# Attention, a Sinkhorn mixture of experts and a top-1 mixture: half blocks in two passes in the second mixture's expert layers, with wider weight splits and moved transposes

## Chip, cores and metric

One core of one Trainium2 chip. The metric is the device time in microseconds of one execution, as the median of several runs. The profile is of one execution, whose own time is given beside its span.

## What is computed

The reference, cut to what matters here: a windowed attention gives `x` (1536 tokens of 512), a first mixture of 8 experts with Sinkhorn weights gives a new `x`, and the second mixture sends each token to one expert:

```python
# attention: B, H, S, D = 2, 8, 768, 64, window 128 with 4 sinks
x = moe_sinkhorn(x)                     # N, D, E, F = 1536, 512, 8, 1024
logits = x @ w_gate
expert_idx = np.argmax(logits, axis=1)
gate_w = softmax(logits)[np.arange(N), expert_idx]
for e in range(E):
    mask = expert_idx == e
    h = np.maximum(x[mask] @ w1[e], 0.0)          # 512 -> 1024
    out[mask] = gate_w[mask, None] * (h @ w2[e])  # 1024 -> 512
```

## The kernel before, in words

The precision of a float32 product is reached with fp32r matmuls: each operand is split into a high part (a rounded copy) and a low part (the rest). `mm3` (line 65) computes a product in three passes, low x high, high x low and high x high, all added up in one PSUM bank.

Attention runs to about 200 us of the span and the first mixture to about 1230 us. In the last part of the first mixture, jobs that run beside its matmuls (`start`, `tick`) route the tokens of the second one: `route_tile` and `route_chunk` find the expert of each token, `pick` takes the fullest expert of the first third of the tokens, `first_tables` fills its two blocks of 128 tokens, and `route_dynamic` (line 569) lays out everything else on VectorE, when all tokens are routed.

The second mixture works on blocks of 128 gathered tokens, called items. Items 0 and 1 belong to the fullest expert. After them come 5 pairs of items (`NPAIR`), each pair with one expert's weights, and 6 single items (`NONE`), each with weights of its own, in the order single, pair, single, pair, and so on: items 2, 5, 8, 11, 14 and 17 are singles, 3 and 4 a pair. These 18 items (`NSURE`) always run; those whose place no tokens need still cost the same. One more single stands behind `tc.If(more == 1)` at the end (line 1448) and runs only when the tokens need it. Which expert an item has is known only at run time: the load's address is read from `ex_i` by SP.

For each item, `gather` (line 695) fetches rows of `x2d` by an indirect DMA from GpSimd, `xs_trans` (703) transposes them on TensorE, ScalarE writes the high part and VectorE the low one. `m2_l1` (714) computes one half (512 columns) of the first layer, and its result is evicted with the ReLU by ScalarE (half 0) or VectorE (half 1). `h_trans` (730) transposes the result in 2 x 4 pieces, again with a high part by ScalarE (L740) and a low part by VectorE (L741). `m2_l2` (744) computes the second layer in 8 steps of three matmuls; ScalarE scales by the gate weight (L757) and an indirect DMA scatters the rows into `out` (L758).

An expert's weights are 4 tiles of 1 MB. SP loads them into 4 raw buffers (`item_load`, line 796). `item_split` and `w_split` (155) split a tile in four pieces of 512 columns, a ScalarE copy (L166) and a VectorE subtraction (L168) each, into one of 7 slots (`SLOTS`, line 128). When a tile is split, the load of the tile four places later starts. `spend(n)` (line 766) issues n pieces, and stops early where the next tile's slot still has matmuls to come; `ensure` issues what a matmul cannot do without. The order is written out by hand, on each engine as the program says (`manual_schedule`):

```python
for i in range(2, NSURE):           # line 1426; shortened
    drain(m2_l1(i + 1, 0)); h_trans(i); gather(i + 3); spend(3)
    drain(m2_l1(i + 1, 1)); spend(3)
    xs_trans(i + 2); spend(3)
    drain(m2_l2(i)); spend(3)
```

Ahead of this loop, items 0 to 2 run with `tick()` between their steps; a job `early(16)` issues split pieces from there, and `spend(8)` stands just before the loop.

Of the kernel before, what the change touches and what calls it, by code (L numbers as in the profile page):

```python
# [23 lines left out]
def kernel(  # L24
# [30 lines left out]
    NITEM = NSURE + 1  # L55
    LAST = 2 * NPAIR + NONE
    ND = 2 * (LAST // 2 + 1)

# [47 lines left out]
    FIRST = {0: 0, 1: 0, NSURE: NSURE}  # L106
    COL = {NSURE: LAST}
    for u in range(NONE):
        FIRST[2 + 3 * u] = 2 + 3 * u
        COL[2 + 3 * u] = 2 * NPAIR + u  # L110
    for t in range(NPAIR):
        for j in range(2):
            FIRST[3 + 3 * t + j] = 3 + 3 * t
            COL[3 + 3 * t + j] = 2 * t + j

# [8 lines left out]
    SEQ += [(NSURE, r) for r in range(4)]  # L124
# [30 lines left out]
    def w_split(p, pool_lo=0):  # L155
        sl, r = w_slot(p)
        th, tl = (f"xh{r}", f"xl{r}") if sl == "x" else (f"wh{sl}{r}", f"wl{sl}{r}")
        h = pools[sl].tile([128, FB, 512], F32R, name=th)
        l = pools[sl].tile([128, FB, 512], F32R, name=tl)
        w_t[p] = h, l  # L160
        raw = raw_t.pop(p)
        for j in range(FB):
            if j == FB - 1 and pool_lo:
                nc.vector.tensor_copy(h[:, j, :], raw[:, j, :])
# [3 lines left out]
            eng.tensor_tensor(l[:, j, :], raw[:, j, :], h[:, j, :].bitcast(F32), op=ALU.subtract)  # L168
            yield
# [392 lines left out]
    def dyn_consts():  # L562
        sk = pools["s"]
        dynj["thr"] = sk.tile([128, NT], F32, name="thr")
        iota(dynj["thr"], [[128, NT]], 0, 0)
        dynj["j"] = sk.tile([128, ND + 1], F32, name="jio")
        iota(dynj["j"], [[128, ND + 1]], 0, 0)

    def route_dynamic():
        sk, psb = pools["s"], pools["ps"]  # L570
        thr, jio = dynj["thr"], dynj["j"]
        re = sk.tile([128, E], F32, name="re")
        nc.vector.tensor_tensor(re, counts, s8, op=ALU.subtract)
        shb = [128, E, NT]
        gt = sk.tile(shb, F32, name="gt")
        nc.vector.tensor_tensor(
            gt, re.unsqueeze(2).to_broadcast(shb), thr.unsqueeze(1).to_broadcast(shb), op=ALU.is_gt
        )
        ds = sk.tile([128, 2, E], F32, name="ds")
        nb = sk.tile([128, E], F32, name="nb")  # L580
        nc.vector.tensor_reduce(ds[:, 0, :], gt[:, :, 1::2], axis=AX.X, op=ALU.add)
        nc.vector.tensor_reduce(nb, gt, axis=AX.X, op=ALU.add)
        nc.vector.scalar_tensor_tensor(ds[:, 1, :], ds[:, 0, :], -2.0, nb, op0=ALU.mult, op1=ALU.add)
        see = [128, 2, E, E]
        tn = sk.tile(see, F32, name="x2h")
        nc.vector.tensor_tensor(
            tn, t8.unsqueeze(1).to_broadcast(see), ds.unsqueeze(2).to_broadcast(see), op=ALU.mult
        )
        ci = sk.tile([128, 2, E], F32, name="ci")
        nc.vector.tensor_reduce(ci, tn, axis=AX.X, op=ALU.add)  # L590
        yield
        d, s1, di = ds[:, 0, :], ds[:, 1, :], ci[:, 0, :]
        dt = sk.tile([128, 4], F32, name="dt")
        nc.vector.tensor_reduce(dt[:, 0:1], di, axis=AX.X, op=ALU.max)
        nc.vector.tensor_scalar(dt[:, 1:2], dt[:, 0:1], 2.0, float(2 * NPAIR), op0=ALU.mult, op1=ALU.max)
        nc.vector.tensor_scalar(dt[:, 2:3], dt[:, 0:1], 2.0, -2.0 * LAST, op0=ALU.mult, op1=ALU.add)
        pv_, al, hi = (sk.tile([128, E], F32, name=nm) for nm in ("sp", "sal", "shi"))
        nc.vector.scalar_tensor_tensor(pv_, ci[:, 1, :], dt[:, 1:2], s1, op0=ALU.add, op1=ALU.subtract)
        nc.vector.tensor_scalar(al, pv_, 2.0, dt[:, 2:3], op0=ALU.mult, op1=ALU.add)
        nc.vector.tensor_scalar(hi, al, float(2 * NPAIR), float(LAST), op0=ALU.is_ge, op1=ALU.mult)  # L600
        nc.vector.tensor_tensor(al, al, hi, op=ALU.max)
        nc.vector.tensor_tensor(al, al, pv_, op=ALU.subtract)
        nc.vector.scalar_tensor_tensor(hi, pv_, float(LAST), al, op0=ALU.is_ge, op1=ALU.mult)
        nc.vector.tensor_tensor(pv_, pv_, hi, op=ALU.add)

        b0, b1, b2 = (sk.tile([128, E], F32, name=nm) for nm in ("b0", "b1", "b2"))
        nc.vector.tensor_scalar(b1, di, 256.0, None, op0=ALU.mult)
        nc.vector.scalar_tensor_tensor(b0, d, -256.0, b1, op0=ALU.mult, op1=ALU.add)
        nc.vector.tensor_scalar(pv_, pv_, 128.0, 65536.0, op0=ALU.mult, op1=ALU.add)
        nc.vector.tensor_tensor(b2, pv_, s1, op=ALU.mult)  # L610
        nc.vector.tensor_scalar(b2, b2, -65536.0, None, op0=ALU.add)
        se = [128, ND, E]
        jb = jio[:, 0:ND].unsqueeze(2).to_broadcast(se)
        g0 = sk.tile(se, F32, name="g0")
        g1 = sk.tile(se, F32, name="g1")
# [8 lines left out]
        nc.vector.tensor_scalar(mo_i, ex[:, LAST:LAST + 1], 0.5, None, op0=ALU.is_gt)  # L624
        nc.vector.tensor_scalar(ex, ex, -1.0, float(E), op0=ALU.mult, op1=ALU.add)
        nc.vector.tensor_scalar(ex_i, ex, float(E - 1), None, op0=ALU.min)
        for n in range(4, 8):
            item_load(n)
        start(early(16), 10)
# [21 lines left out]
        sg = [128, NT, ND + 1]  # L651
        G = sk.tile(sg, F32, name="G")
        nc.vector.tensor_tensor(
            G, sd.unsqueeze(2).to_broadcast(sg), jio.unsqueeze(1).to_broadcast(sg), op=ALU.is_ge
        )
        jn = sk.tile([128, NT], F32, name="jn")
        nc.vector.tensor_reduce(jn, G[:, :, 1:ND + 1], axis=AX.X, op=ALU.add)
        nc.vector.scalar_tensor_tensor(sd, jn, -128.0, sd, op0=ALU.mult, op1=ALU.add)
        yield
        J = G[:, :, 0:ND]  # L660
        nc.vector.tensor_tensor(J, J, G[:, :, 1:ND + 1], op=ALU.subtract)
        nh = NT // 2
        sj = [128, nh, ND]
        As = [sk.tile([128, nh, 3, ND], F32R, name=nm) for nm in ("x2h", "x2l")]
        for u, A in enumerate(As):
            us = slice(u * nh, (u + 1) * nh)
            for j, g in enumerate((idp1[:, us], ghl[:, us, 0].bitcast(F32), ghl[:, us, 1].bitcast(F32))):
                eng = nc.gpsimd if u == 1 and j > 0 else nc.vector
                eng.tensor_tensor(A[:, :, j, :], J[:, us], g.unsqueeze(2).to_broadcast(sj), op=ALU.mult)
        tp = psb.tile([128, 3 * ND], F32, name="tabd", tag="m1")  # L670
        Rs = [onehots(sd[:, c * TPC:(c + 1) * TPC]) for c in range(2)]
        yield 2
        for c in range(NC):
            cols = [As[b // nh][:, b % nh].rearrange("p j e -> p (j e)") for b in range(c * TPC, (c + 1) * TPC)]
            place(tp, Rs[c], cols, c == 0, c == NC - 1)
            if c + 2 < NC:
                Rs.append(onehots(sd[:, (c + 2) * TPC:(c + 3) * TPC]))
            if c == 1:
                yield 1
        finish(tp, ND, ig_d, is_d, g_d)  # L680
        for i in range(2, 5):
            gather(i)

# [3 lines left out]

    def index(st, dy, i):
        return st[:, i:i + 1] if i < 2 else dy[:, COL[i]:COL[i] + 1]

# [4 lines left out]
    def gather(i):  # L695
# [3 lines left out]
            out=x, out_offset=None, in_=src, in_offset=bass.IndirectOffsetOnAxis(ap=index(ig_s, ig_d, i), axis=0)  # L699
# [3 lines left out]
    def xs_trans(i):  # L703
        x = xs_t.pop(i)
        tp = pools["ps"].tile([128, KD, 128], F32, name="xst", tag="m0")
        for kk in range(KD):
            nc.tensor.transpose(tp[:, kk, :], x[:, kk * 128:(kk + 1) * 128], ident)
# [4 lines left out]
        xst[i] = th, tl  # L712

    def m2_l1(i, hf):
# [5 lines left out]
        for kk in range(KD):  # L720
            mm3(ps, th[:, kk, :], tl[:, kk, :], wh[:, kk, :], wl[:, kk, :], kk == 0, kk == KD - 1)
# [22 lines left out]
    def m2_l2(i):  # L744
        pool, tag = ((ps_m, "y0"), (pools["ps"], "m2"))[i % 2]
        ps = pool.tile([128, DM], F32, name="y", tag=tag)
        for f in range(2 * FB):
# [4 lines left out]
            mm3(ps, th[:, f % FB, :], tl[:, f % FB, :], wh[:, f % FB, :], wl[:, f % FB, :], f == 0, f == 2 * FB - 1)  # L752
# [738 lines left out]
```

## Time and profile before

| what | value |
|---|---|
| median of 3 runs | 1462.15 us (1461.98 to 1463.06) |
| the profiled execution | 1461.6 us |
| its span, first to last instruction | 1459.8 us |
| TensorE busy, share of the span | 98% |
| VectorE, ScalarE, GpSimd busy | 47%, 31%, 9% |
| mean granted TensorE clock | 0.995 of full speed |

The span is what the profiler saw of the program; the time is longer by the start and the end of the execution. Matmuls are pipelined, so that the duration of one (some 390 ns) is longer than the step from one to the next. PE is TensorE, PEld its weight loads, DVE VectorE, ACT ScalarE, POOL GpSimd, SP the engine that issues the loads; a "q" behind the name is the engine's queue.

### The profile page before, as it was taken

To read this page: it belongs to the slowest core of one execution; us is meant where nothing else is said; L and a number is where in the kernel's file an instruction comes from. 1 tells how busy PE (TensorE), PEld (TensorE's weight loads), DVE (VectorE), ACT (ScalarE), POOL (GpSimd) and SP (SyncE) were. 2 spreads that over 40 slices of the span, in tenths; PEclk is the share of its full clock that TensorE was granted. 3 is DMA by queue.
4 is the path that set the end of the run, shared out by engine and by line. 5 is a ranking of instruction groups with operands and counts; after the bars stand their busy time and mean duration, and the time that the engine had idled before them with its cause. 6 is when DMAs were issued, how large, how long until landed. Compare 5 with 4: busy or idle time off the path is not lost. (4 is left out here: it accounts for less than half of the span.)

```text
span 1459.8 us, 18270 instructions
## 1 busy us (share of the span) xinstructions
PE 1426.6 (98%) x7181; PEld 1169.4 (80%) x7181; DVE 687.8 (47%) x1445; ACT 457.9 (31%) x974; POOL 125.5 (9%) x164
## 2 busy tenths in 40 slices
PE   7799999999999999999999999999999998999998
PEld 5587887888888888888888888888888876788886
DVE  7677644543333323233333323243333367877774
ACT  5766522021121212022111202112111132766664
POOL 3644400000000000000000000000000000111111
PEclk9999999999999999999999999999999999999999
DMA  6322112010101001010100001010100041977771
GB/s 131 76 59 53 37 58 87 0 58 1 58 8 51 29 29 58 1 58 0 58 30 29 29 30 58 0 58 1 58 1 0 30 144 44 352 278 266 267 256 52
DMA packets 86026, 105.64 MB, mean 72 GB/s; under 512 B 41519, under 2 KB 41519, under 8 KB 85937
## 3 DMA queue, kind: packets, MB, share of 16 engines
q1 hardware_dynamic: 83056, 96.58, 20.3%
q0 software_dynamic: 2880, 7.87, 1.6%
q8 instruction: 57, 0.93, 0.3%
q14 instruction: 33, 0.26, 0.1%
HBM read 101.29 MB, written 7.86 MB: 75 GB/s over the span
## 5 line engine op out<-in xcount | busy, mean ns | idle before, releaser
L201 ACT ACTIVATE hh<-L 128x512 fp32r<-128x512 f32 x192 | 114.7, 597 | 794.9 <-PE L L68 794.8
L202 DVE SCALAR_TENSOR_TENSOR hl<-L,hh 128x512 fp32r<-128x512 f32 x192 | 132.7, 691 | 345.6 <-ACT hh L201 344.9
L226 DVE SCALAR_TENSOR_TENSOR acc<-y,Pm,acc 128x512 f32<-128x512 f32 x168 | 126.1, 751 | 252.3 <-PE y L68 251.9
L66 PE MATMUL y<-whb,hl 128*128 128x512 f32 x432 | 170.7, 395 | 0.0
L68 PE MATMUL y<-whb,hh 128*128 128x512 f32 x432 | 168.5, 390 | 0.0
L67 PE MATMUL y<-wlb,hh 128*128 128x512 f32 x432 | 168.1, 389 | 0.0
L66 PE MATMUL y<-wha,hl 128*128 128x512 f32 x412 | 162.9, 395 | 0.0
L68 PE MATMUL y<-wha,hh 128*128 128x512 f32 x412 | 160.5, 390 | 0.0
L67 PE MATMUL y<-wla,hh 128*128 128x512 f32 x412 | 160.4, 389 | 0.0
L66 PE MATMUL L<-xh,wla 128*128 128x512 f32 x384 | 152.3, 397 | 0.0
L66 PE MATMUL L<-xh,wlb 128*128 128x512 f32 x384 | 151.0, 393 | 0.0
L68 PE MATMUL L<-xh,wha 128*128 128x512 f32 x384 | 149.6, 390 | 0.0
L68 PE MATMUL L<-xh,whb 128*128 128x512 f32 x384 | 149.6, 389 | 0.0
L67 PE MATMUL L<-xl,wha 128*128 128x512 f32 x384 | 149.6, 389 | 0.0
L67 PE MATMUL L<-xl,whb 128*128 128x512 f32 x384 | 149.5, 389 | 0.0
L68 PEld LDWEIGHTS y<-whb,hh 128*128 128x128 f32 x432 | 81.1, 188 | 17.3
L67 PEld LDWEIGHTS y<-wlb,hh 128*128 128x128 f32 x432 | 81.2, 188 | 16.0
L66 PEld LDWEIGHTS y<-whb,hl 128*128 128x128 f32 x432 | 81.1, 188 | 16.0
L698 POOL DMA_INDIRECT acc<-x2d,ig_s x2 | 2.1, 1052 | 1044.7 <-DVE tmp_d L449 1019.6
L68 PEld LDWEIGHTS y<-wha,hh 128*128 128x128 f32 x412 | 77.3, 188 | 16.3
L66 PEld LDWEIGHTS y<-wha,hl 128*128 128x128 f32 x412 | 77.3, 188 | 16.3 <-issue 0.3
L67 PEld LDWEIGHTS y<-wla,hh 128*128 128x128 f32 x412 | 77.4, 188 | 15.0
(311 smaller groups left out, 2328.6 us busy)
## 6 DMA issues: line engine op xcount, KB each, us to landing
raw<-in_moe_w SPq DMA_DIRECT2D x80, 1024.0 KB
raw<-in_v SPq DMA_DIRECT2D x12, 256.0 KB
raw<-vfb SPq DMA_DIRECT2D x12, 256.0 KB
x2d<-acc SPq DMA_DIRECT2D x12, 256.0 KB
raw<-in_k SPq DMA_DIRECT2D x11, 256.0 KB
raw<-in_q SPq DMA_DIRECT2D x11, 256.0 KB
raw<-in_k SPq DMA_DIRECT2D x2, 128.0 KB
raw<-in_q SPq DMA_DIRECT2D x2, 128.0 KB
```

What stands on the lines that cost most here:

```text
L66: nc.tensor.matmul(out_ap, al, bh, start=start, stop=False)
L67: nc.tensor.matmul(out_ap, ah, bl, start=False, stop=False)
L68: nc.tensor.matmul(out_ap, ah, bh, start=False, stop=stop)
L201: nc.scalar.activation(hh, ps, AF.Relu)
L202: nc.vector.scalar_tensor_tensor(hl, ps, 0.0, hh.bitcast(F32), op0=ALU.max, op1=ALU.subtract)
L226: nc.vector.scalar_tensor_tensor(a, ps, Pm[:, blk, e:e + 1], a, op0=ALU.mult, op1=ALU.add)
L698: nc.gpsimd.indirect_dma_start(out=x, out_offset=None, in_=src, in_offset=bass.IndirectOffsetOnAxis(ap=index(ig_s, ig_d, i), axis=0))
```

## The change

Of the 6 single items the last five (5, 8, 11, 14, 17) become half items of 64 rows. A half item's high and low parts lie side by side in one tile, 64 columns each, so that one matmul gives high rows in partitions 0 to 63 and low rows in 64 to 127; two passes, with the low and the high part of the weights, take the place of three, and `both` adds the two halves of the bank. The ReLU of a half item moves behind the transposes. The gather, the transposes and the scatter of a half item have 64 rows.

Routing counts remainders over 128 (a pair), over 64 (a full single) and up to 64 (a half). What does not fit goes to up to five pairs in nested branches at the end, in place of the one single; for this the tables are made by functions that can run again (`table_experts`, `tables`; their operations are those of before, with 16 columns instead of 18).

Weight tiles from the fifth on are split in two pieces of 1024 columns. The transposes of item i + 1 are issued inside the second layer of item i, after 5 of its 8 steps. The diff, cut to its core:

```diff
+    NHALF = NONE - 1
+    NOVER = 5
+    NITEM = NSURE + 2 * NOVER
+    ND = 2 * NPAIR + NONE
+    HALF = {2 + 3 * u for u in range(1, NONE)}
...
-    def w_split(p, pool_lo=0):
+    def w_split(p, pool_lo=0, n=1):
...
-        for j in range(FB):
+        for j in range(0, FB, n):
+            js = slice(j, j + n)
...
-                nc.scalar.activation(h[:, j, :], raw[:, j, :], AF.Copy)
+                nc.scalar.activation(h[:, js, :], raw[:, js, :], AF.Copy)
...
     def xs_trans(i):
...
+        n = rows(i)
+        tp = pools["ps"].tile([128, KD, 128], F32, name="xst", tag="m0")[:, :, 0:n]
         for kk in range(KD):
+            nc.tensor.transpose(tp[:, kk, :], x[0:n, kk * 128:(kk + 1) * 128], ident[0:n, 0:n])
+        if i in HALF:
+            st = stile("xsh", i, [128, KD, 128], F32R)
+            nc.scalar.activation(st[:, :, 0:n], tp, AF.Copy)
+            nc.vector.tensor_tensor(st[:, :, n:128], tp, st[:, :, 0:n].bitcast(F32), op=ALU.subtract)
+            xst[i] = st, None
+            return
...
+    def mm(out_ap, ah, al, bh, bl, start, stop):
+        if al is not None:
+            mm3(out_ap, ah, al, bh, bl, start, stop)
+        else:
+            nc.tensor.matmul(out_ap, ah, bl, start=start, stop=False)
+            nc.tensor.matmul(out_ap, ah, bh, start=False, stop=stop)
+
+    def both(dst, ps):
+        nc.scalar.activation(dst, ps[64:128, :], AF.Copy)
+        nc.vector.tensor_tensor(dst, ps[0:64, :], dst, op=ALU.add)
...
     def m2_l1(i, hf):
...
-        if hf == 0 or i < 2 or i == NSURE - 1:
+        if i in HALF:
+            both(h[0:64, :], ps)
+        elif hf == 0 or i < 2 or i == NSURE - 1:
...
     def h_trans(i, hfs=(0, 1)):
...
+            if i in HALF:
+                hi = th[:, :, 0:n]
+                nc.scalar.activation(hi, tp, AF.Relu)
+                nc.vector.scalar_tensor_tensor(
+                    th[:, :, n:128], tp, 0.0, hi.bitcast(F32), op0=ALU.max, op1=ALU.subtract
+                )
...
     def m2_l2(i):
...
+        if i in HALF:
+            both(y, ps)
+            ps = y
         nc.scalar.activation(y, ps, AF.Copy, scale=index(g_s, g_d, i))
...
-        start(early(16), 10)
+        start(early(8), 10)
...
     def early(n):
         for _ in range(n):
             spend(1)
-            yield 1
+            yield 2
...
-        yield from w_split(P1 + n)
+        yield from w_split(P1 + n, n=1 if n < 4 else 2)
...
         while jobs:
             tick()
-        spend(8)
+        h_trans(2)
+        spend(4)
         for i in range(2, NSURE):
             if i + 1 < NSURE:
                 drain(m2_l1(i + 1, 0))
-                h_trans(i)
             if i + 3 < NSURE:
                 gather(i + 3)
-            if not tail:
-                spend(3)
+            spend(2 if i % 3 == 0 else 1)
             if i + 1 < NSURE:
                 drain(m2_l1(i + 1, 1))
-            spend(3)
+            spend(2)
             if i + 2 < NSURE:
                 xs_trans(i + 2)
-            if not tail:
-                spend(3)
+            spend(1)
             for n, _ in enumerate(m2_l2(i)):
-                if tail and n == 4:
+                if n == 4 and i + 1 < NSURE:
                     h_trans(i + 1)
-                    spend(16)
-            spend(3)
+            spend(1 if i < NSURE - 2 else 8)
-        more = nc.values_load(mo_i[0:1, 0:1], min_val=0, max_val=1)
-        with tc.If(more == 1):
+        more = nc.values_load(mo_i[0:1, 0:1], min_val=0, max_val=NOVER)
+        def over(t):
+            if t == NOVER:
+                return
+            with tc.If(more > t):
...
+                over(t + 1)
```

In `route_dynamic`, the arithmetic from the counts to `ex_i` goes from 32 VectorE operations to 29; after the gathers of items 2 to 4, five more compute the number of overflow pairs.

## Rows read from the trace of the kernel before

**Rows 1.** The page, busy tenths of 40 slices of the span:

```profile
PE   7799999999999999999999999999999998999998
GB/s 131 76 59 53 37 58 87 0 58 1 58 8 51 29 29 58 1 58 0 58 30 29 29 30 58 0 58 1 58 1 0 30 144 44 352 278 266 267 256 52
```

**Rows 2.** Busy time by stretch: stretch, us, engines, PEclk, DMA share, GB/s

```profile
1240.00:1260.00 20.00, 18.95 (x85) 14.85 (x86) 16.86 (x43) 10.80 (x20) 5.89 (x8) 0.91 0.94 335
1260.00:1280.00 20.00, 20.00 (x102) 16.77 (x101) 18.57 (x31) 17.11 (x34) 2.77 (x3) 1.00 0.98 346
...
1360.00:1380.00 20.00, 20.00 (x100) 16.67 (x99) 12.59 (x21) 12.38 (x24) 4.22 (x4) 1.00 0.75 260
```

**Rows 3.** Waits of PE, 1215 to 1460: us, times, longest; first and last of six

```profile
PE L L66 <- DVE acc L711: 2.0, 1, 2.0
...
PE rkp L409 <- DVE oh_all L402: 0.2, 1, 0.2
```

**Rows 4.** Timeline of PE: start us, us, engine, line, operation, out<-in, count

```profile
1437.97 0.60 PE L737 MATMUL h2p<-ident,hh 128*128 128x128 f32 x4
...
1438.77 0.47 PE L66 MATMUL L<-xh,acc 128*128 128x512 f32 x1
...
1450.66 0.39 PE L66 MATMUL y<-whb,hl 128*128 128x512 f32 x1
...
1453.16 0.39 PE L68 MATMUL y<-whb,hh 128*128 128x512 f32 x1
```

**Rows 5.** Timeline of POOL, two scatters of neighbouring items

```profile
1350.41 1.01 POOL L758 DMA_INDIRECT out<-acc,is_d  x1 [9.88 <-ACT acc L757]
...
1362.71 1.01 POOL L758 DMA_INDIRECT out<-acc,is_d  x1 [9.88 <-ACT acc L757]
```

**Rows 6.** Timeline of PE, matmuls with 54 moving columns

```profile
1247.55 0.74 PE L533 MATMUL tabd<-x2h,acc 128*128 128x54 f32 x6
1248.13 0.38 PE L533 MATMUL tabd<-x2l,acc 128*128 128x54 f32 x2
```

**Rows 7.** Timeline of DVE, first operation of the layout and the eviction behind it

```profile
1232.51 0.15 DVE L573 TENSOR_TENSOR re<-counts,s 128x8 f32<-128x8 f32 x1
...
1239.62 0.68 DVE L711 TENSOR_TENSOR acc<-xst,acc 128x512 fp32r<-128x512 f32 x1
```

**Rows 8.** Groups by line and shape, whole span: busy us, mean ns, idle before

```profile
L1019 DVE TENSOR_TENSOR xl<-pv,xh 64x256 fp32r<-64x256 f32 x48 | 20.0, 416 | 14.9 <-ACT xh L1206 13.7 <-PE tr L1158 0.6 <-PE L L1028 0.2
L1089 DVE TENSOR_TENSOR vsk<-acc,vsk 64x512 fp32r<-64x512 f32 x2 | 1.4, 686 | 0.4 <-ACT vsk L1088 0.4
L1088 ACT ACTIVATE vsk<-acc 64x512 fp32r<-64x512 f32 x2 | 1.2, 616 | 0.0
```

**Rows 9.** Timeline of all engines, end of item 2's first layer

```profile
1262.94 0.39 PE L68 MATMUL L<-whb,acc 128*128 128x512 f32 x1
...
1263.37 0.69 DVE L728 TENSOR_SCALAR hl<-L 128x512 f32<-128x512 f32 x1
```

**Rows 10.** Groups by line and shape, 1240 to 1460

```profile
L168 DVE TENSOR_TENSOR xl<-raw,xh 128x512 fp32r<-128x512 f32 x76 | 48.3, 683 | 16.1 <-ACT xh L166 16.1
L166 ACT ACTIVATE xh<-raw 128x512 fp32r<-128x512 f32 x76 | 42.2, 631 | 0.7 <-DMA raw<-in_moe_w 0.7
...
L741 DVE TENSOR_TENSOR hl<-h2p,hh 128x512 fp32r<-128x512 f32 x34 | 22.0, 686 | 13.7 <-ACT hh L740 13.7
```

**Rows 11.** Timeline of all engines, the end of the span

```profile
1453.63 0.69 ACT L757 ACTIVATE acc<-y,g_d 128x512 f32<-128x512 f32 x1 [4.80 <-PEq L1448]
1454.59 0.98 POOL L758 DMA_INDIRECT out<-acc,is_d  x1 [4.50 <-ACTq L1448]
```

**Rows 12.** Busy time by stretch, the landing of the last scatter

```profile
1455.00:1459.00 4.00, 0.00 (x0) 0.00 (x0) 0.00 (x0) 0.00 (x0) 0.57 (x1) 0.62 0.06 20
```

**Rows 13.** Instructions of the early branch, line 923, on DVE's queue

```profile
L923 DVEq COMPARE_BRANCH  x1: 67/67/67, 7.7 to 7.7; - x1
L923 DVEq EVENT_SEMAPHORE  x1: 21/21/21, 8.3 to 8.3; - x1
```

More of the change, by code (lines that the diff above doesn't have):

```diff
@@ L113 @@
             FIRST[3 + 3 * t + j] = 3 + 3 * t
-            COL[3 + 3 * t + j] = 2 * t + j
+            COL[3 + 3 * t + j] = NONE + 2 * t + j
+    for t in range(NOVER):
+        for j in range(2):
+            FIRST[NSURE + 2 * t + j] = NSURE + 2 * t
+            COL[NSURE + 2 * t + j] = 2 * t + j
+    HALF = {2 + 3 * u for u in range(1, NONE)}
     def whose(i, rs):
@@ L123 @@
     NHEAD = len(SEQ)
-    SEQ += [(NSURE, r) for r in range(4)]
+    SEQ += [(NSURE + 2 * t, r) for t in range(NOVER) for r in range(4)]
     place_of = {ir: n for n, ir in enumerate(SEQ)}
@@ new lines, in dtile @@
+        def dtile(shape, nm):
+            dynj[nm] = pools["s"].tile(shape, F32, name=nm)
+            return dynj[nm]
+        thr = dtile([128, 3, NT // 2], "thr")
+        for j, a in enumerate((128, 64, 0)):
+            iota(thr[:, j, :], [[256, NT // 2]], a, 0)
+        iota(dtile([128, ND + 1], "jio"), [[128, ND + 1]], 0, 0)
+        for j, (n, a, b) in enumerate(((1, 511, 514 + NONE - 6), (NHALF, 512, 506 + NONE - 6))):
+            for nm, x in (("lim", n), ("pb", 128 * a), ("cv", 128 * b)):
+                t = dtile([128, 2, E], nm) if j == 0 else dynj[nm]
+                nc.gpsimd.memset(t[:, j, :], float(x))
@@ L616, in route_dynamic, with table_experts @@
+    def table_experts(b0, b1, b2, off):
+        sk = pools["s"]
+        se = [128, ND, E]
+        jb = dynj["jio"][:, 0:ND].unsqueeze(2).to_broadcast(se)
+        g0 = sk.tile(se, F32, name="lgs0")
+        g1 = sk.tile(se, F32, name="lgs1")
+        if off:
+            for b in (b0, b1, b2):
+                nc.vector.tensor_scalar(b, b, -off, None, op0=ALU.add)
         nc.vector.tensor_tensor(g0, jb, b0.unsqueeze(1).to_broadcast(se), op=ALU.is_ge)
@@ L623, in route_dynamic, with tables @@
         nc.vector.tensor_reduce(ex, g0, axis=AX.X, op=ALU.add)
-        nc.vector.tensor_scalar(mo_i, ex[:, LAST:LAST + 1], 0.5, None, op0=ALU.is_gt)
         nc.vector.tensor_scalar(ex, ex, -1.0, float(E), op0=ALU.mult, op1=ALU.add)
         nc.vector.tensor_scalar(ex_i, ex, float(E - 1), None, op0=ALU.min)
+    def tables(sd):
+        sk, psb = pools["s"], pools["ps"]
+        jio = dynj["jio"]
+        sg = [128, NT, ND + 1]
+        G = sk.tile(sg, F32, name="G")
+        nc.vector.tensor_tensor(
+            G, sd.unsqueeze(2).to_broadcast(sg), jio.unsqueeze(1).to_broadcast(sg), op=ALU.is_ge
+        )
+        jn = sk.tile([128, NT], F32, name="jn")
+        nc.vector.tensor_reduce(jn, G[:, :, 1:ND + 1], axis=AX.X, op=ALU.add)
+        sr = sk.tile([128, NT], F32, name="sr")
+        nc.vector.scalar_tensor_tensor(sr, jn, -128.0, sd, op0=ALU.mult, op1=ALU.add)
+        yield
+        J = G[:, :, 0:ND]
+        nc.vector.tensor_tensor(J, J, G[:, :, 1:ND + 1], op=ALU.subtract)
+        nh = NT // 2
+        sj = [128, nh, ND]
+        As = [sk.tile([128, nh, 3, ND], F32R, name=nm) for nm in ("x2h", "x2l")]
+        for u, A in enumerate(As):
+            us = slice(u * nh, (u + 1) * nh)
+            for j, g in enumerate((idp1[:, us], ghl[:, us, 0].bitcast(F32), ghl[:, us, 1].bitcast(F32))):
+                eng = nc.gpsimd if u == 1 and j > 0 else nc.vector
+                eng.tensor_tensor(A[:, :, j, :], J[:, us], g.unsqueeze(2).to_broadcast(sj), op=ALU.mult)
+        tp = psb.tile([128, 3 * ND], F32, name="tabd", tag="m1")
+        Rs = [onehots(sr[:, c * TPC:(c + 1) * TPC]) for c in range(2)]
+        yield 2
+        for c in range(NC):
+            cols = [As[b // nh][:, b % nh].rearrange("p j e -> p (j e)") for b in range(c * TPC, (c + 1) * TPC)]
+            place(tp, Rs[c], cols, c == 0, c == NC - 1)
+            if c + 2 < NC:
+                Rs.append(onehots(sr[:, (c + 2) * TPC:(c + 3) * TPC]))
+            if c == 1:
+                yield 1
+        finish(tp, ND, ig_d, is_d, g_d)
@@ L680, in route_dynamic @@
-        finish(tp, ND, ig_d, is_d, g_d)
+        yield from tables(sd)
         for i in range(2, 5):
             gather(i)
+        mo = sk.tile([128, 2], F32, name="mo")
+        nc.vector.tensor_scalar(mo[:, 0:1], mx[:, 2:3], mx[:, 1:2], -float(NHALF), op0=ALU.subtract, op1=ALU.add)
+        nc.vector.tensor_scalar(
+            mo[:, 1:2], vb[:, 1, 0:1], 1.0 / 256, -0.5 * (506 + NONE - 6) - NPAIR, op0=ALU.mult, op1=ALU.add
+        )
+        nc.vector.scalar_tensor_tensor(mo[:, 0:1], mo[:, 0:1], 0.0, mo[:, 1:2], op0=ALU.max, op1=ALU.add)
```

193 lines of the change are left out of this document (86 added, 107 removed).

## The prediction

> **What bounds the kernel now.** I read the page's slices first, then the busy time by stretch, the waits, and the timeline of the last stage. The slices [rows 1] show TensorE at 9 tenths nearly throughout. The change touches only what comes after about 1232 us: the token routing and the second expert layer. In that stage TensorE is busy for the whole 20 us of each stretch [rows 2], at full granted clock, but for 1240:1260. From 1215 us on the view of waits lists six of TensorE, from 2.0 to 0.2 us, under 5 us together [rows 3], and in the stretches from 1260 to 1440 us none. So the stage is bound by TensorE's instruction stream: what leaves it is saved, as long as weights, splits and evictions keep up.
>
> Matmuls overlap, so their price is the pitch, not the 390 ns of a row: eleven steps from 1450.66 to 1453.16 give 0.2273 us each [rows 4]. Two output scatters stand 12.30 us apart [rows 5], one block: 48 matmuls x 0.2273 = 10.9 us, the rest twelve transposes (eight take 0.80 us [rows 4]) and their edges.
>
> **The change part by part.**
>
> *Two passes instead of three.* Five of the 18 blocks (5, 8, 11, 14, 17) become 64 rows. High and low part lie side by side as 128 stationary columns, so each product takes two matmuls of 512 moving columns, same shape as now. First layer 8 products, second 8: 16 matmuls fewer per block (3.64 us, so 8.66 us instead of 12.3), 80 in all, 80 x 0.2273 = **-18.2 us**, all on the path.
>
> *Narrower transposes.* Each half block's 12 transposes write 64 columns. No row shows that. Matmuls with 54 moving columns behind full 128-column weights still step by 0.58/6 = 0.097 us [rows 6], against 0.80/8 = 0.10 here. Halving would save 0.05 each. I take 0.01, by the nearest row: 60 x 0.01 = **-0.6 us** (bounds 0 and -3.0). [...]
>
> *Routing arithmetic.* The chain of VectorE before the next block's eviction runs from 1232.51 to 1239.62, 7.1 us and 32 small operations [rows 7]; TensorE's 2.0 us wait for the eviction L711 hangs on it. The new chain has 29, some wider (144 and 192 columns instead of 96 and 128), the six table operations narrower (128 instead of 144): **-0.3 us** (bounds -0.8 and +0.5). Five operations for the overflow count come after the gathers, on VectorE, 0.2 us each: beside TensorE; their only cost is in the next term. The clock fell to half in 1240:1260 (0.91 granted [rows 2]) right after that wait: some eight matmuls at twice the pitch, about 1.6 us. I leave it; not falling would be a gain of 1.6.
>
> *Hidden transposes moved.* Now block i's transposes come after one half of block i+1's first layer; then, they come inside block i-1's second layer, after five of its eight steps. Same instructions, and TensorE waits at none now, so nothing is gained. What is late next: they need both halves of the first layer evicted. Behind its last matmul stand a transpose group (0.44 us) and 15 matmuls (10 in a half block), 3.85 us (2.7), and the eviction takes 0.62 + 0.69 us on a half block [rows 8], plus at most two split pieces queued before it on VectorE, 2.4 us. It fits, narrowly at a half block. Block 2 has no earlier block to hide in: its transposes follow its own first layer at once. That layer's last matmul starts at 1262.94, VectorE's eviction at 1263.37 and takes 0.69 [rows 9]: ready at 1264.1, wanted at 1263.6 after the first half's four transposes: 0.5 us of wait, up to 1.5 with a longer split piece in front. **+0.8 us** (0.3 to 1.5).
>
> *Splits by 1024 columns.* 44 loads of 1 MB are split as before, in two pairs instead of four. A 512 column piece takes 0.683 us on VectorE and 0.631 on ScalarE [rows 10]; the longer one saves at most some 0.1 us, on engines off the path. Price: an eviction may wait up to 0.6 us longer behind a piece. It matters only where TensorE has no cover, before block 2: **+0.4 us** (0 to 1). Splits come at the same rate against the blocks (16 pieces per three blocks, as many as are used), later by up to half a load's.
>
> *The end.* The last block is a half. Now the last matmul starts at 1453.16, ScalarE's scaling at 1453.63, the scatter at 1454.59 [rows 4, 11]. A ScalarE copy and a VectorE add of 64x512 (0.616 and 0.686 us [rows 8]) come before the scaling: **+1.3 us** (1.2 to 1.6). The skipped block's branch stays; the scatter's 64 rows instead of 128 I price at 0.
>
> *Weights.* 44 MB-size loads at the 346 GB/s of 1260:1280 [rows 2] take 133 us, from 1240 to about 1375 if never held up; the last one is needed near 1430. Four raw buffers and seven split slots stay. Later stretches moved 260 GB/s at a share of 0.75 [rows 2]; 8 loads per three blocks take 24.3 us of the new 33.2 (2 x 12.3 + 8.66). ScalarE waited 0.7 us for loads in the largest group [rows 10]. No cost.
>
> *VectorE.* Per three blocks (two full, one half): splits 32 x 0.60 (its pitch is the 0.683 less the overlap of 0.08) = 19.2, the full blocks 2 x 2.4, the half some 2.85 (0.42 for 256 columns, 0.69 for 512 [rows 8], less overlap): 26.9 of 33.2 us. Not the bound, if handoffs overlap.
>
> Sum: -18.2 - 0.6 - 0.3 + 0.8 + 0.4 + 1.3 = -16.6. The profiled execution took 1461.6 (span 1459.8): 1445.0. The median of the runs, 1462.15, is 0.5 above it: **1445.5 us**.
>
> **Rivals.** *VectorE behind ScalarE.* The split groups idled before VectorE's part: 16.1 us over 76 pieces, 0.21 each, and 13.7 over 34 transposed halves, 0.40 each [rows 10]. Were that idle time unavoidable, three blocks would need 26.9 + 32 x 0.21 + 4 x 0.40 = 35.2 us, 2 more than TensorE, some 10 over five rounds: 1455.5. For it: a busy share of 0.81 and longer pieces. Against: with 12.3 us per block those waits were slack that VectorE had to spend somewhere; in 1260:1280 it was busy 18.57 of 20 us [rows 2] and TensorE did not wait.
>
> *A block of overflow runs.* The tokens must fit 5 pairs, one full and five half blocks. If one remainder too many is over 64, a pair is computed at the end with nothing beside it: tables again (some 10 us, of which [rows 7] show 7.1 for the first part), 4 loads (12.2 us), 96 matmuls and 24 transposes (24.4), some 11 us of bare evictions: +58, **1503 us**, slower. It decides at one token too many. Against: the reference's gate, on the inputs it draws, sends the eight experts 4, 67, 558, 544, 50, 129, 145 and 39 tokens. The fixed first two blocks take 256 of one of the large ones; the remainders are 5 pairs (129, 145, and 3 from the large ones), one of 67, five of at most 50: it fits exactly. The trace agrees: the last scatter moved 20 GB/s for 4 us, 80 KB, 39 rows of 2 KB [rows 12]. For it: only another set of inputs.
>
> *The branch over five nested pairs.* The skipped code grows from one block to ten with tables. At the early branch L923 VectorE reached the far side 0.6 us after the compare [rows 13]. If ScalarE or GpSimd, which branch last, had to fetch their far side after the scatter, the end would move by two to four such steps: +2 us, 1447.5. [...] Against: GpSimd skips few instructions, and the scatter's landing gives 4 us of cover.
>
> **How the numbers follow.** Forecast 0.75; VectorE 0.14; branch 0.05; overflow 0.04; the rest (gains eaten by waits I do not see) 0.02. Low end: transposes halved (-2.4), no clock fall (-1.6), block 2's wait at 0.3 (-0.5): 1441. High end: most of VectorE's case, 1454. The measurement tells 0.2% (2.9 us) from no change. Faster holds the forecast, the branch and VectorE's case, less a little for VectorE at twice its price: 0.92; slower is the overflow, 0.04; same 0.04.
>
> **What the changed profile would show.** Right: scatters of full and half blocks 12.3 and about 8.5 us apart; 80 fewer 512 column matmuls at an unchanged 0.227; one wait of TensorE at block 2's transposes of 0.5 to 1.5 us; three operations instead of one between last matmul and last scatter. Wrong: TensorE waiting each round for an eviction or a split (VectorE's case), matmuls after the final branch (overflow), a gap between last scatter and end that grew (branch), or waits of ScalarE for loads after 1300 us.

## The result, and the profile after

The changed kernel takes 1447.67 us (median of 4 runs, 1447.51 to 1448.78), the kernel before 1462.08 (4 runs, 1461.98 to 1463.06): a ratio of 0.9902 (95% interval 0.9884 to 0.9919), 14.4 us less. The forecast was 1445.5; the measured time lies inside its range of 1441 to 1454. The profiled execution took 1447.51 us, its span 1445.3; the comparison below is with the profiled 1461.6 of before.

The page's slices and the stretches of the same times as in [rows 1, 2] come first; of the stretches the columns are span, busy time of PE, PEld, DVE, ACT and POOL, granted clock, DMA share, GB/s.

```profile
PE   7799999999999999999999999999999999899997
GB/s 131 78 59 53 38 59 87 1 59 1 59 0 59 29 29 30 29 59 0 58 0 59 30 30 30 30 58 0 58 1 0 15 161 37 248 319 276 271 291 71
```

```profile
1240.00:1260.00 20.00, 17.67 (x89) 13.91 (x88) 16.32 (x37) 10.89 (x15) 6.22 (x7) 1.00 1.02 370
1260.00:1280.00 20.00, 19.60 (x96) 16.12 (x96) 17.08 (x19) 14.77 (x21) 2.41 (x3) 1.00 0.94 325
...
1360.00:1380.00 20.00, 20.00 (x100) 16.41 (x99) 14.67 (x19) 14.06 (x21) 3.36 (x3) 1.00 0.84 296
...
1300.23:1333.50 33.27, 33.27 (x166) 27.20 (x165) 26.22 (x30) 24.44 (x34) 7.37 (x6) 1.00 0.75 270
```

TensorE is still the bound from 1280 us to its last matmul at 1435: busy for the whole of every stretch at full clock. Two things differ in 1240:1260: the clock no longer falls there (1.00, it was 0.91), and yet TensorE works less of the time (17.67 us of 20, it was 18.95). The waits of TensorE from 1215 us on say why (total, times, longest):

```profile
PE xst L755 <- DMA acc<-x2d,ig_d: 2.0, 1, 2.0
PE L L67 <- DVE acc L766: 1.5, 1, 1.5
...
PE h2p L808 <- DVE hl L798: 0.4, 1, 0.4
```

The wait for the eviction behind the routing arithmetic went from 2.0 [rows 3] to 1.5 us; a wait for item 2's gather, 0.3 us before, has grown to 2.0; item 2's transposes wait 0.4 us, as forecast in kind. GpSimd's timeline has the gather itself and one round of three scatters:

```profile
1248.01 1.01 POOL L745 DMA_INDIRECT acc<-x2d,ig_d  x1 [4.18 <-DVE tmp_d L458]
...
1300.23 1.01 POOL L841 DMA_INDIRECT out<-acc,is_d  x1 [7.69 <-ACT acc L840]
...
1312.23 0.94 POOL L841 DMA_INDIRECT out<-acc,is_d  x1 [9.27 <-ACT acc L840]
...
1323.07 1.01 POOL L841 DMA_INDIRECT out<-acc,is_d  x1 [8.07 <-ACT acc L840]
...
1333.50 1.01 POOL L841 DMA_INDIRECT out<-acc,is_d  x1 [7.64 <-ACT acc L840]
```

Three blocks take 1333.50 - 1300.23 = 33.27 us. Before, three blocks of this stage took 36.88 (scatters at 1301.24 and 1338.12): 3.61 less per round, where 16 x 0.2273 is 3.64. The single intervals are 12.00, 10.84 and 10.43, not "12.3 and about 8.5". Between two scatters lie the second layer of one block and the first layer of the block after it, so a half block takes 8 x 0.2273 = 1.8 us from each of two intervals. Its own scatter (the one of 0.94 us, at 1312.23) also comes later behind its last matmul, by the copy and the add (1.38 us in the table below): the interval that ends at it grows by that, the next one shrinks by it. An estimate from these numbers is 10.5 for the interval ahead of these two, 11.9 and 10.9, where 10.43, 12.00 and 10.84 were measured.

The end of the span, timeline of all engines:

```profile
1435.01 0.39 PE L774 MATMUL y<-whb,hh 128*128 128x512 f32 x1
1435.48 0.59 ACT L778 ACTIVATE acc<-y 64x512 f32<-64x512 f32 x1 [2.94 <-PE y L774]
1436.11 0.68 DVE L779 TENSOR_TENSOR acc<-y,acc 64x512 f32<-64x512 f32 x1 [5.60 <-ACT acc L778]
1436.82 0.72 ACT L840 ACTIVATE acc<-acc,g_d 64x512 f32<-64x512 f32 x1 [0.75 <-DVE acc L779]
1437.82 0.93 POOL L841 DMA_INDIRECT out<-acc,is_d  x1 [4.01 <-ACTq L1531]
```

Cut at four marks that both traces have, the difference of the profiled executions is as follows. The first mark is a matmul of the routing (`rkp`, L409 before and L418 after), the second the first matmul of item 2's first layer. TensorE's timeline before:

```profile
1228.07 0.28 PE L409 MATMUL rkp<-oh_all,trir 128*128 128x32 f32 x1 [0.21 <-DVE oh_all L402]
...
1257.12 0.50 PE L66 MATMUL L<-xh,acc 128*128 128x512 f32 x1
```

After:

```profile
1227.47 0.28 PE L418 MATMUL rkp<-oh_all,trir 128*128 128x32 f32 x1 [0.19 <-DVE oh_all L411]
...
1256.30 0.50 PE L67 MATMUL L<-xh,acc 128*128 128x512 f32 x1
```

| stretch | before | after | difference |
|---|---|---|---|
| start to that matmul of the routing (`rkp`; TensorE's work unchanged) | 1228.07 | 1227.47 | -0.60 |
| from there to the first matmul of item 2's first layer | 29.05 | 28.83 | -0.22 |
| from there to the start of the last matmul | 196.04 | 178.71 | -17.33 |
| last matmul to last scatter | 1.43 | 2.81 | +1.38 |
| last scatter to the end of the span | 5.21 | 7.48 | +2.27 |
| span to the execution's time | 1.80 | 2.21 | +0.41 |

The sum is -14.09, as 1447.51 - 1461.6. The first row is no effect of the change that these runs show: over all the changed kernels below, that mark lies between 1227.4 and 1229.0. The stage gained what was forecast within a microsecond; 2.27 us were lost behind the last scatter, where the forecast had priced nothing. On GpSimd's queue at the last branch (count: shortest/median/longest ns, first and last start) the two kernels differ. Before:

```profile
L1448 POOLq COMPARE_BRANCH  x1: 45/45/45, 1454.8 to 1454.8; - x1
L1448 POOLq EVENT_SEMAPHORE  x1: 17/17/17, 1455.0 to 1455.0; - x1
L1448 POOLq INC_SWDGE_SEM  x1: 917/917/917, 1455.1 to 1455.1; - x1
```

After:

```profile
L1531 POOLq EVENT_SEMAPHORE  x5: 17/42/1935, 1438.2 to 1440.5; - x5
L1531 POOLq COMPARE_BRANCH  x1: 45/45/45, 1438.1 to 1438.1; - x1
L1531 POOLq INC_SWDGE_SEM  x1: 900/900/900, 1440.5 to 1440.5; - x1
```

Where one event of 17 ns stood there are five, one of 1935 ns, and the INC_SWDGE_SEM behind them (an instruction of GpSimd's queue that stands there where the skipped body holds GpSimd transfers) starts 2.4 us after the branch instead of 0.3. From its start to the end of the span it is 4.7 us before and 4.8 after: what delayed it delayed the end.

### The profile page after: what moved, and what is told of

It reads as the page before. It is cut to its first block, busy times and chain, and to the rows that moved or that the text cites. A ratio compares the mean times of both kernels' runs of the same rounds, so it can differ in the third digit from the quotient of the medians.

```text
span 1445.3 us, 17989 instructions
## 1 busy us (share of the span) xinstructions
PE 1406.3 (97%) x7101; PEld 1150.3 (80%) x7101; DVE 684.6 (47%) x1369; ACT 454.1 (31%) x895; POOL 130.2 (9%) x172
## 5 line engine op out<-in xcount | busy, mean ns | idle before, releaser
L67 PE MATMUL y<-whb,hl 128*128 128x512 f32 x416 | 164.8, 396 | 0.0
L69 PE MATMUL y<-whb,hh 128*128 128x512 f32 x416 | 162.2, 390 | 0.0
L68 PE MATMUL y<-wlb,hh 128*128 128x512 f32 x416 | 162.1, 390 | 0.0
L69 PEld LDWEIGHTS y<-whb,hh 128*128 128x128 f32 x416 | 78.1, 188 | 16.6
L67 PEld LDWEIGHTS y<-whb,hl 128*128 128x128 f32 x416 | 78.1, 188 | 15.7
L68 PEld LDWEIGHTS y<-wlb,hh 128*128 128x128 f32 x416 | 78.2, 188 | 15.3
```

What stands on the lines that cost most here:

```text
L67: nc.tensor.matmul(out_ap, al, bh, start=start, stop=False)
L68: nc.tensor.matmul(out_ap, ah, bl, start=False, stop=False)
L69: nc.tensor.matmul(out_ap, ah, bh, start=False, stop=stop)
```

## Experiments

All times are medians, with a ratio to the kernel before that ran on the same chip. "The stage" is the third row of the table above, "the end chain" the fourth, "the end gap" the fifth.

**No half blocks** (`e1_nohalf`): every single is a full block again; routing, splits, order and branches stay changed.

```diff
-    HALF = {2 + 3 * u for u in range(1, NONE)}
+    HALF = set()
```

> The five half blocks are full blocks again (128 rows, three passes); everything else of the change stays. If the stage is bound by TensorE's stream, as forecast, five blocks get 16 matmuls back, 5 x 3.63 = +18.1 us, the end loses the copy and the add (-1.4): 1447.7 + 18.1 - 1.4 = 1464.4 us, two more than the kernel before, since the other parts of the change cost a little. If VectorE or the supply of weights already held the changed kernel up, the half blocks gave less than that: below 1461 us. If the moved transposes or the wider splits brought part of the gain, also below 1462.

Measured: 1465.18 us (10 runs), ratio 1.0020 (1.0011 to 1.0030). The rest of the change is a loss of 3 us. In its profiled execution the stage is 196.70 us, so the half blocks are worth 196.70 - 178.71 = 17.99 of the 80 x 0.2273 = 18.2; the end chain is back at 1.43, and the end gap is 7.52: that loss is not the half blocks'. Its stage is 0.66 us longer than the 196.04 of before, which the moved transposes account for with 0.4 (next experiment).

**The transposes where they were** (`e2_htrans_old`): `h_trans(i)` again behind half 0 of the next first layer.

```diff
-        h_trans(2)
         spend(4)
...
                 drain(m2_l1(i + 1, 0))
+                h_trans(i)
...
-                if n == 4 and i + 1 < NSURE:
+                if n == 4 and i == NSURE - 2:
```

> The transposes of a block's first layer stand again behind the first half of the next block's first layer. If their place does not matter, only block 2's wait of 0.4 us goes: 1447.3 us. If half blocks leave them too little cover (a half block's second half of the first layer and one transpose group, 2.3 us, against about 2.0 us of evictions plus split pieces queued ahead), TensorE waits up to 1 us in each of five rounds: up to 1452 us. My forecast priced the move at nothing, so it expects 1447.3.

Measured: 1447.95 us, 0.9904 (0.9887 to 0.9920): no difference that can be told. Item 2's 0.4 us wait is gone and the stage 0.39 us shorter (178.32); the gather's wait is 0.4 us longer (2.4). In the steady state TensorE waits in neither kernel. The move is worth nothing there, and costs item 2 its 0.4 us.

**Splits of 512 columns** (`e3_split512`): pieces of the old width, twice as many at each `spend`.

```diff
-        yield from w_split(P1 + n, n=1 if n < 4 else 2)
+        yield from w_split(P1 + n, n=1)
...
-            spend(2 if i % 3 == 0 else 1)
+            spend(4 if i % 3 == 0 else 2)
```

> Splits go in four pieces of 512 columns again, at the same rate. If TensorE's stream is the bound, 1447.7 within 0.5 us. If VectorE is near the bound (it is busy some 0.8 of the last stage), the finer pieces cost it about 0.06 us each pair, 5 us in all, and the time rises by 1 to 5 us.

Measured: 1448.75 us, 0.9907 (0.9890 to 0.9924). The stage is 178.67 us, the changed kernel's to 0.04, and a round takes 33.26. Of the profiled execution's 1.87 us more, 1.56 lie ahead of `rkp` (1229.03 instead of 1227.47), where this edit changes nothing that TensorE does, and 0.34 between there and item 2, where the granted clock fell to 0.83 in 1220:1240 (1.00 in the changed kernel). The width of a piece is worth nothing to TensorE, though it does save engine time off the path: after the change a split group reads

```profile
L177 DVE TENSOR_TENSOR xl<-raw,xh 128x1024 fp32r<-128x1024 f32 x38 | 45.5, 1220 | 12.8 <-ACT xh L175 12.8
L175 ACT ACTIVATE xh<-raw 128x1024 fp32r<-128x1024 f32 x38 | 38.7, 1052 | 0.8 <-DMA raw<-in_moe_w 0.8
```

1220 ns where two of 683 were needed, and 1052 for two of 631 [rows 10].

**One overflow pair** (`e4_over1`), **two** (`e5_over2`), and **five whose transfers come from SP** (`e6_over5_sp`). The first two shorten the skipped code; the third leaves it long, and takes its gathers and scatters off GpSimd (the second cut below, in `gather` and in `m2_l2`).

```diff
-    NOVER = 5
+    NOVER = 1      # e4; 2 in e5
```

```diff
         src = x2d[0:2 * CH, :] if i == 0 else x2d
+        if i >= NSURE:
+            nc.sync.dma_start(x, x2d[0:128, :])
+            xs_t[i] = x
+            return
...
         nc.scalar.activation(y, ps, AF.Copy, scale=index(g_s, g_d, i))
+        if i >= NSURE:
+            nc.sync.dma_start(out[0:128, :], y)
+            return
```

> One overflow pair instead of five behind the last branch (not taken with these inputs, either way); fewer tokens could overflow. In the changed kernel the span ends 7.5 us after the last scatter starts, 5.2 before, with a wait of 1.9 us on GpSimd's queue at the branch. If that wait is for the landing of the last scatter, because five pairs hold 20 GpSimd transfers on 8 queue semaphores so that the skipping path must bring all eight up to date, one pair with 4 transfers does not touch the last scatter's semaphore: end gap 5.3 us, 1445.5 us. If it is the distance of the branch (code to fetch), the gap falls as well, in proportion to the skipped code: this run alone does not tell the two apart, the next two do.

> Two overflow pairs instead of five. They hold 8 GpSimd transfers, one on each of the 8 queue semaphores, the last scatter's among them. If the wait at the branch is for that scatter's landing, it stays whole: 7.5 us from the last scatter to the end, 1447.7 us. If it is the distance of the branch, two fifths of the skipped code leave some 0.9 of the 2.3 us: 1446.3 us.

> Five overflow pairs as in the change, but their gathers and scatters (never executed with these inputs) are plain transfers of fixed rows on SP's queue, so that the skipped code is as long but holds no GpSimd transfer; with an overflow the output would be another. If the wait at the branch is for the last scatter's landing, it goes: 5.2 us or less from the last scatter to the end, 1445.3 us or less. If it is the distance of the branch, it stays: 7.5 us, 1447.7 us.

Measured: one pair 1446.95 us, 0.9897 (0.9880 to 0.9913), end gap 5.39; two pairs 1447.79, 0.9899 (0.9881 to 0.9917), end gap 7.43; five by SP 1445.81, 0.9883 (0.9865 to 0.9900), end gap 4.82. The profiles separate what the medians only hint at. GpSimd's queue at the branch, one pair:

```profile
L1531 POOLq EVENT_SEMAPHORE  x3: 17/17/43, 1439.0 to 1439.2; - x3
...
L1531 POOLq INC_SWDGE_SEM  x1: 909/909/909, 1439.3 to 1439.3; - x1
```

Two pairs:

```profile
L1531 POOLq EVENT_SEMAPHORE  x5: 17/43/1933, 1438.8 to 1441.0; - x5
...
L1531 POOLq INC_SWDGE_SEM  x1: 900/900/900, 1441.1 to 1441.1; - x1
```

Five pairs, transfers by SP:

```profile
L1538 POOLq COMPARE_BRANCH  x1: 45/45/45, 1438.9 to 1438.9; - x1
L1538 POOLq EVENT_SEMAPHORE  x1: 17/17/17, 1439.1 to 1439.1; - x1
```

The cost doesn't grow with the skipped code: two pairs have all of it (an end gap of 7.43, where five have 7.48), five pairs without GpSimd's transfers none (4.82). It is a step, between one pair (5.39) and two. A pair holds four GpSimd transfers (two gathers, two scatters), and the program's instruction listing spreads GpSimd's transfers over eight queue semaphores: one pair touches four of them (`DMASW4` to `DMASW7` in the listing), two pairs all eight, among them the one that the last scatter signals (`DMASW3`). The one single of the kernel before touches two others (`DMASW4` and `DMASW5`). In the listings of these kernels GpSimd's path past the branch waits for each semaphore that the skipped body would have used, so in the two with two pairs or more that use GpSimd it waits for the last scatter to land: that wait stands there in the changed kernel and in `e5_over2`, and in neither `e4_over1` nor `e6_over5_sp`. The time of the wait agrees: the INC_SWDGE_SEM starts 2.7 us after the scatter's issue in both (1440.5 - 1437.82 and 1441.1 - 1438.37), and the DMA queues, in the changed kernel, moved bytes until 1439.8, 0.7 us before it (stretches of the end, columns as above):

```profile
1439.00:1440.00 1.00, 0.00 (x0) 0.00 (x0) 0.00 (x0) 0.00 (x0) 0.00 (x0) 0.50 0.36 80
1440.00:1441.00 1.00, 0.00 (x0) 0.00 (x0) 0.00 (x0) 0.00 (x0) 0.00 (x0) 0.50 0.00 0
```

**A full block last** (`e7_last_full`): the one full single goes to the end, item 2 becomes a half.

```diff
-    HALF = {2 + 3 * u for u in range(1, NONE)}
+    HALF = {2 + 3 * u for u in range(NONE - 1)}
...
-        COL[2 + 3 * u] = u
+        COL[2 + 3 * u] = (u + 1) % NONE
```

`h_trans(2)` comes behind half 0 of item 3's first layer here.

> The full single block goes last (17) and the first single (2) is a half; block 2's transposes stand behind the first half of block 3's first layer. The end then has one operation between the last matmul and the last scatter instead of three: -1.4 us; block 2's wait of 0.4 us goes as well: 1445.9 us. If the shorter block 2 runs into weights that are still under way (ScalarE waited 0.8 us for loads near 1268), TensorE waits there 1 to 2 us and the gain is gone: 1447.5.

Measured: 1449.14 us, 0.9906 (0.9888 to 0.9923): no faster than the changed kernel (0.9902), where a gain was expected. The end did what was expected (the end chain is 1.44 instead of 2.81), but item 2 starts 1.62 us later behind `rkp` (at 1258.43, 30.45 behind it) and the stage is 1.19 longer (179.90). Its stretches behind the gather's wait (2.4 us here) show the clock:

```profile
1254.00:1258.00 4.00, 2.88 (x9) 2.32 (x10) 1.25 (x2) 1.33 (x2) 0.00 (x0) 0.59 1.02 367
1258.00:1262.00 4.00, 4.00 (x13) 3.12 (x12) 2.07 (x3) 2.60 (x4) 2.06 (x2) 0.56 0.89 328
```

In these 8 us the granted clock was 0.59 and 0.56, and TensorE's steps took about twice as long: thirteen from 1255.71 to 1261.42 take 5.71 us, 0.44 each instead of 0.23. The loss of some 2.7 us is more than the 1.37 that the end gave back. But this is one execution: the kernel's four took 1448.24 to 1450.71 us at a mean granted clock of 0.996 to 0.992, and the one at 0.996 lies within the range of the changed kernel, whose four all stood at 0.996. It is not that a wait of 2.4 us always does this; `e2_htrans_old` waited as long in the same place and kept 1.00 in 1240:1260. What tips it stays open, and so does what the order is worth at an equal clock.

**Two loads behind the gather** (`e8_late_loads`): of the four weight loads that start ahead of the gather, two start behind it.

```diff
-        for n in range(4, 8):
+        for n in range(4, 6):
             item_load(n)
...
+        for n in range(6, 8):
+            nc.gpsimd.memset(raw2[n % 4][:, 0, 0:1], 0.0)
+            item_load(n)
```

> Two of the four first weight loads of the routed blocks start behind block 2's gather instead of ahead of it (a tiny write by GpSimd to their raw buffers holds them; nothing else changes). If block 2's gather lands late because it shares the transfer engines with 4 MB of loads, it lands some 3 us earlier and TensorE's wait of 2.0 us at block 2's transposes goes: 1445.7 us. If the weights themselves are then late, ScalarE waits for loads some 3 us longer near 1268, and TensorE behind it: 1447 to 1449. If the gather was late for another reason, nothing moves: 1447.7.

Measured: 1450.69 us, 0.9914 (0.9896 to 0.9932); its four runs, 1449.98 to 1450.84, all lie above the changed kernel's. The gather, issued at 1249.35, is there when TensorE comes at 1253.44, 4.09 us later (6.25 in the changed kernel). TensorE's wait for it is gone and item 2 starts 27.03 us behind `rkp` instead of 28.83, 1.8 earlier. But then the waits of 1240 to 1270 read

```profile
PE h2p L812 <- DVE hl L802: 2.6, 1, 2.6
ACT whb L175 <- DMA raw<-in_moe_w: 1.6, 1, 1.6
ACT wha L175 <- DMA raw<-in_moe_w: 1.4, 1, 1.4
```

ScalarE's splits wait for the late weights, VectorE's behind them, an eviction behind those, and TensorE 2.6 us for that. Behind this wait the clock falls too:

```profile
1264.00:1268.00 4.00, 2.90 (x10) 2.42 (x11) 2.85 (x5) 2.09 (x3) 0.00 (x0) 0.69 1.05 364
```

The stage takes 182.91 us, 4.2 more: 2.2 by the longer wait (2.6 for 0.4), and 1.6 by the clock, since the eight steps behind the wait take 3.50 us (1265.52 to 1269.02) where they take 1.91 in the changed kernel (1263.78 to 1265.69). The gather does wait among the loads, and the loads are needed.

**The scale folded into the sum** (`e9_fuse`), and the same with **one overflow pair** (`e10_fuse_over1`):

```diff
-            both(y, ps)
-            ps = y
-        nc.scalar.activation(y, ps, AF.Copy, scale=index(g_s, g_d, i))
+            g = index(g_s, g_d, i)
+            nc.scalar.activation(y, ps[64:128, :], AF.Copy, scale=g)
+            nc.vector.scalar_tensor_tensor(y, ps[0:64, :], g, y, op0=ALU.mult, op1=ALU.add)
+        else:
+            nc.scalar.activation(y, ps, AF.Copy, scale=index(g_s, g_d, i))
```

> A half block's scaling is folded into its two halves' sum: ScalarE copies the lower half of the bank with the scale, VectorE multiplies the upper half by the gate weight and adds. One 64x512 ScalarE operation (0.72 us in the changed kernel) goes from the path at the end, five times in all, four of them beside other work. If the end chain is serial, last matmul to last scatter falls from 2.81 to about 2.1 us, and the time by 0.7, to about 1446.9. If the scatter is held by something else (its index, its queue), the 2.81 stays. The gap from last scatter to the span's end stays at 7.4 to 7.5 us, the wait for the landing being counted from the scatter.

> The same, and one overflow pair behind the final branch instead of five. If the two costs at the end are independent, both go: chain 2.1 us, last scatter to end 5.4 us (as with one pair alone), 2.8 us below the changed kernel, about 1444.9. If the wait of the skipping path had only hidden another one of the same length behind the scatter, the gap stays above 7 us and the time is that of the folded scaling alone, 1446.9.

Measured: 1447.31 us, 0.9905 (0.9888 to 0.9921), and 1445.11 us (1444.62 to 1445.96), 0.9885 (0.9868 to 0.9901). The end of the second:

```profile
1435.66 0.39 PE L774 MATMUL y<-whb,hh 128*128 128x512 f32 x1
1436.14 0.69 ACT L839 ACTIVATE acc<-y,g_d 64x512 f32<-64x512 f32 x1 [2.99 <-PEq L1533]
1436.86 0.74 DVE L840 SCALAR_TENSOR_TENSOR acc<-y,g_d,acc 64x512 f32<-64x512 f32 x1 [5.75 <-ACTq L1533]
1437.88 0.93 POOL L843 DMA_INDIRECT out<-acc,is_d  x1 [3.46 <-DVE acc L840]
```

Two operations instead of three, 0.69 and 0.74 us where 0.59, 0.68 and 0.72 stood: 2.22 us to the scatter, 0.6 less, and the end gap is 5.42. The two costs of the end are independent and both go. This version has the lowest median, 2.2 us below `e9_fuse` on the same chip, and all its runs lie below all of the changed kernel's; its ratio can't be told from that of `e6_over5_sp` (0.9883), whose overflow pairs compute nothing of use. Its price is room for one overflow pair instead of five. The folded scale alone shows in the trace (0.6 us) but not in the medians.

## Why the prediction was right, and where it was not

The kernel is faster, as forecast, and by the mechanism forecast: the stage is TensorE's stream, and removing 80 matmuls removes 80 pitches (-18.2; 17.99 in the stage with and without half blocks, 3.61 per round). By the forecast's own terms:

**Narrower transposes, -0.6: no gain, by the rows a loss of some 0.5.** On TensorE's timeline the steps inside the longer group did shrink:

```profile
1428.46 0.39 PE L69 MATMUL y<-wha,hh 128*128 128x512 f32 x1
1428.78 0.46 PE L808 MATMUL h2p<-ident,hh 64*128 64x64 f32 x4
1429.08 0.41 PE L808 MATMUL h2p<-ident,hl 64*128 64x64 f32 x4
1429.42 0.50 PE L67 MATMUL y<-wha,hl 128*128 128x512 f32 x1
1429.75 0.39 PE L68 MATMUL y<-wla,hh 128*128 128x512 f32 x1
```

From the first of the eight to the next matmul it is 0.64 us, where full ones took 0.80 [rows 4]: 0.16 less. But the edges took it back: 0.32 us from the last matmul to the first transpose, where full ones have a pitch of 0.23. From the matmul ahead to the second one behind, the eight take 1429.75 - 1428.46 = 1.29 us, and full ones of the same kernel 1.34 (1318.67 to 1320.01). The four transposes of the gathered rows even lose:

```profile
1314.65 0.39 PE L69 MATMUL L<-wha,acc 128*128 128x512 f32 x1
1314.97 0.46 PE L755 MATMUL xst<-ident,acc 64*128 64x64 f32 x4
...
1315.70 0.39 PE L68 MATMUL y<-xl,hh 128*128 128x512 f32 x1
```

That is 1.05 us, where full ones take 0.90 (1325.26 to 1326.16). So a half block gains 0.05 and loses 0.15: some 0.1 us more per block, 0.5 over five by this estimate, where the forecast took off 0.6 with bounds of 0 and -3.0. The time of a round shows no gain either (3.61, the matmuls alone being 3.64).

**Routing, -0.3, and the clock's fall, left as it was.** The chain from L646 to the eviction L766 now runs from 1231.92 to 1238.66, 6.74 us against 7.11 [rows 7]: -0.37, as forecast. The clock did not fall (1.00 in 1240:1260, before 0.91), though that isn't shown to be the change's doing: in `e3_split512`, with the same routing, it was 0.83 in 1220:1240. TensorE came earlier: it reached item 2's transposes 24.78 us behind `rkp` instead of 26.67. The forecast had called a clock that doesn't fall a gain of 1.6. It was none: the gather landed 26.79 us behind `rkp`, before 27.01, and this 0.22 is all that was gained. This step of the prediction failed: it looked at what TensorE does there and not at what arrives next: the gather was 0.3 us from the bound already. It was issued 1.5 us earlier than before (20.54 behind `rkp` instead of 22.07) and took 6.25 us from its issue to TensorE's first use, where it had taken 4.94, at 370 GB/s of loads in the same stretch (335 before). `e8_late_loads` shows both halves of it: with two loads less ahead of it the gather took 4.09 us at most, and item 2 started 1.8 us earlier. The rows are, on the timelines of GpSimd and TensorE before:

```profile
1250.14 1.01 POOL L698 DMA_INDIRECT acc<-x2d,ig_d  x1 [5.21 <-DVE tmp_d L449]
...
1255.08 0.63 PE L707 MATMUL xst<-ident,acc 128*128 128x128 f32 x4 [0.34 <-DMA acc<-x2d,ig_d]
```

and after, behind the issue at 1248.01 shown above:

```profile
1254.26 0.63 PE L755 MATMUL xst<-ident,acc 128*128 128x128 f32 x4 [2.01 <-DMA acc<-x2d,ig_d]
```

**Item 2's wait, +0.8: 0.4**, inside the bounds. **Longer pieces before item 2, +0.4:** 0.1; with pieces of the old width (`e3_split512`) the same wait is 0.3 us. The stage lost 0.85 of its 18.2: 0.4 for this wait. Of the other 0.45, 0.19 is what the half blocks lack of 18.18 against `e1_nohalf` (17.99), less than the 0.5 that the rows of the narrower transposes give; the rest isn't assigned.

**The end, +1.3: +1.38**, by the three operations named.

**"The skipped block's branch stays": +2.27.** This is the term with the largest miss: it was put at nothing, and the runs show 2.27 us. The gain was overestimated by 2.5 us (-14.1 for -16.6); the differences of the other terms, from -0.6 in the untouched part to +0.7 in the stage and +0.4 between span and time, nearly cancel. That they cancel is luck; the -0.6 is no effect of the change that the runs show. The prediction's third rival had the size (+2 us, 1447.5) and the sign to look for, a gap behind the last scatter that grew; its cause is refuted. It said that engines pay for a far jump. GpSimd branched at 1438.1 and reached its first event at 1438.2; the time went into a wait for the scatter's landing, which the rival had counted as cover. No run here shows such a price on the path: ten skipped blocks without GpSimd's transfers have an end gap of 4.82, shorter than the 5.21 of one block before.

**Weights, VectorE, no cost:** right. TensorE's stretches from 1280 us on have no wait for weights. VectorE was busy 26.22 us of a round of 33.27 (forecast 26.9 of 33.2) and TensorE never waited for it after item 2, so the idle time in front of its operations was slack; VectorE's rival falls. No overflow ran: nothing follows the last matmul at 1435.01.

## What to carry to other kernels

Where one engine's stream fills the stage, the pitch times the number of instructions removed was a forecast good to 5% here (17.33 us in the stage for 18.2); what is lost lies at the stage's two ends, so price both: what arrives next when the bound engine comes early, and what everything behind the last transfer waits for. A conditional body that is never entered cost 2.27 us here: read in the instruction listing what the skipping path waits for, and keep the last store's semaphore out of it. An edit that only moves or widens work beside the bound (the splits, and the place of the transposes) was worth nothing here, where that engine didn't wait for it: the stage took 178.71 us with both, 178.67 with the old splits, 178.32 with the old place. Narrower work on the bound engine is priced with its edges: the transposes' own steps shrank (0.64 us for eight instead of 0.80), and the time from the matmul ahead to the second one behind hardly did (1.29 instead of 1.34).

## What the runs showed of the hardware that was not expected

- Skipping a body with eight or more GpSimd transfers held GpSimd's queue in one event for 1.93 to 1.99 us in the changed kernel, `e1_nohalf`, `e5_over2` and `e9_fuse`; the end of the span followed 4.7 to 4.8 us behind the INC_SWDGE_SEM in these four, in the kernel before, in `e4_over1` and in `e10_fuse_over1`.
- Eight transposes of 64 columns took 0.64 us, eight of 128 took 0.80, but the step into them was 0.32 us instead of 0.23; four of them took 1.05 us, edges included, where four full ones took 0.90.
- The same gather of 128 rows took 4.94 us to its first use before, 6.25 in the changed kernel, and at most 4.09 in `e8_late_loads`, with only the traffic around it and its moment changed.
- The granted clock around 1230 to 1262 us differs between traces whose TensorE waits there are alike: 1.00 behind a wait of 2.4 us in one, 0.56 to 0.59 in another. It isn't fixed by the kernel: of the four executions of `e3_split512`, two at a mean granted clock of 0.995 took 1448.1 us, two at 0.992 took 1449.4 and 1449.6.
